# Program order on all engines and later weight conversions in a Mamba-2 scan followed by a low-rank mixer

## Chip, cores, metric

One core of a Trainium2 chip. The metric is the device time of one launch in microseconds (us), median of several executions. Each profile shows one execution; its span, from the first to the last instruction, is some 1.7 us shorter than that execution's time. The granted clock of a stretch is the share of TensorE's full speed that was granted in it: 1.00 is full speed. All runs are fast, save one execution that is named where it occurs. Ratios are the mean time of one kernel's fast runs over that of the other's of the same rounds, so not quite the ratio of the medians quoted.

## The reference

Four batches, eight heads, 768 positions. A chunked state-space scan makes y from x, a, B and C; y becomes a (768 x 256) matrix per batch, and a mixer with weights U, V, w1, w2 follows. The weights come as 64-bit floats and are converted to fp32 on the chip.

```
y[chunk] = (C B^T * L) x + (C state) * decay        # scan, per batch and head
state    = decay_full * state + sum(B x * decay_from_j)
h = y^T @ U @ V ;  u = y + h^T                      # mixer, per batch
out = u + relu(u @ w1) @ w2
```

## The kernel before

The scan works on pairs of 128-row chunks: twelve pairs in all, three per batch (NPR = 3), counted from 0, so that the fourth pair is pair 3. For a pair, `prep` scales B and C with decays (Bs, Cs, bd), `turn` transposes them on TensorE (T), `gram` multiplies them, a VectorE mask gives M, `state` carries S and `wide`, `ychannel` forms y, `ytokens` transposes y back (ytok). The mixer of a batch consists of pieces: `project` (ytok with U, gives pT), `mixed` (pT with V, added to yT), sixteen `up` pieces (w1, relu) and six `down` pieces (w2). All pieces but `mixed` (bank "g") put their products into three PSUM banks "w", which the scan uses too.

```python
    def to_fp32(dst, words):                     # one weight of 64-bit words
        ...                                      # (cut: lo, hi, tmp)
        nc.vector.tensor_scalar(out=e, in0=hi, ...)                       # exponent bits
        nc.scalar.activation(power, e, AF.Relu, bias=bias[:p], scale=8.0)
        nc.vector.scalar_tensor_tensor(out=power, in0=hi, ..., in1=power, ...)
        nc.vector.tensor_scalar(out=top, in0=hi, ...)
        nc.vector.tensor_tensor(out=top, in0=top, in1=power, ...)
        nc.vector.scalar_tensor_tensor(out=rest, in0=lo, ..., in1=power, ...)
        nc.gpsimd.tensor_tensor(out=dst, in0=rest, in1=top, op=ALU.add)
    ...
    with tc.manual_schedule(engines={PE}):       # only TensorE keeps program order
        prep(0); turn(0, 0); turn(0, 1); state(0); gram(0); prep(1)
        pieces = [lambda w=w: to_fp32(*w) for w in weights]   # ten conversions
        for k in range(last + 1):
            ...
            if k: ytokens(k - 1)
            if q == 0 and b:
                some(len(pieces))                # all conversions are done here
                pieces = mixer(b - 1)
                some(2)                          # project, mixed
            ...                                  # prep(k+2), turn(k+1), pieces between
            ychannel(k); state(k + 1); gram(k + 1); some(parts[2])
```

## Time and profile before

| | before |
|---|---|
| time, median of 3 (range) | 294.89 us (294.77 to 295.44) |
| first projection (L403), last part starts | 65.35 us |
| batch 1's projection starts | 127.03 us |
| VectorE busy up to the first projection | 48.44 us |
| TensorE busy up to the first projection | 30.01 us, at clock 0.74 |

Busy time must be read by stretch: over the whole span VectorE is busy 37%, which looks harmless; up to 65 us it is 74%.

### The profile page before, as it was taken

Reading aid. Unit: us, or ns where it says so; the run is one execution under the profiler, and the core shown is the slowest. Engines: PE = TensorE matmul, PEld = TensorE weight load, DVE = VectorE, ACT = ScalarE, POOL = GpSimd, SP = SyncE. Lnnn points to the kernel's source line nnn. Section 1 sums busy time; section 2 is a strip of 40 time slices with the busy share of each in tenths; the row PEclk is TensorE's granted clock in tenths of the full one; section 3 lists DMA queues with packets and bytes.
Section 4 is the critical chain, followed back from the end, with each engine's and each line's share of the span. In section 5 each row is a group of like instructions: output and inputs, shape, how many; then the busy total and the mean of one; then the engine's idle time right before and its main releaser. Section 6 shows DMA issues by size and latency. Waiting matters only on the chain.

```text
span 294.8 us, 5144 instructions
## 1 busy us (share of the span) xinstructions
PE 252.9 (86%) x2238; PEld 193.3 (66%) x2238; DVE 109.2 (37%) x196; ACT 57.1 (19%) x114; POOL 50.9 (17%) x68
## 2 busy tenths in 40 slices
PE   4447631819999999999999999999999998999994
PEld 4436411605778768867788688676886785587583
DVE  2339999794530244034401541325005103200100
ACT  5212331201211121122211221122121111101100
POOL 4333539251401113004011040001000000000000
PEclk9776955775999999999999999999999999999999
DMA  7998889899900100010001000100010001001001
GB/s 91 102 193 294 172 152 112 91 119 96 109 0 0 56 1 2 0 56 2 0 2 53 2 2 0 54 2 2 0 53 2 0 2 53 0 2 53 0 0 53
DMA packets 80950, 14.65 MB, mean 50 GB/s; under 512 B 76000, under 2 KB 79264, under 8 KB 80928
## 3 DMA queue, kind: packets, MB, share of 16 engines
q1 hardware_dynamic: 80928, 14.33, 28.6%
q8 instruction: 17, 0.28, 0.4%
q14 instruction: 5, 0.04, 0.1%
HBM read 11.17 MB, written 3.15 MB: 49 GB/s over the span
## 4 chain that ended last, share of the span: by engine, by line
PE 77%; DVE 9%; SPq 7%; DMA 3%; issue 1%; POOL 1%; ACT 1%; DVEq 0%; POOLq 0%
PE w L424 29%; PE w L440 28%; PE y L374 4%; PE g L310 3%; PE y L367 3%; SPq L94 3%; SPq L93 2%; DVE M L315 2%; PE w L297 2%; DMA words<-in_moe_U_dram 2%; SPq L97 2%; PE w L436 2%; PE w L403 2%; DVE rest L247 2%; PE g L413 2%; DVE power L240 1%
## 5 line engine op out<-in xcount | busy, mean ns | idle before, releaser
L424 PE MATMUL w<-yT,w 128*128 128x384 f32 x256 | 88.7, 497 | 1.1 <-DVE yT L417 1.1
L440 PE MATMUL w<-w,gT 128*128 128x256 f32 x384 | 86.9, 379 | 0.0
L440 PEld LDWEIGHTS w<-w,gT 128*128 128x128 f32 x384 | 71.1, 190 | 8.7
L424 PEld LDWEIGHTS w<-yT,w 128*128 128x128 f32 x256 | 48.0, 193 | 32.0 <-DVE yT L417 2.7
L427 DVE TENSOR_SCALAR gT<-w 128x384 f32<-128x384 f32 x32 | 17.8, 557 | 62.3 <-PE w L424 62.3
L315 DVE TENSOR_TENSOR M<-g,causal 128x1024 int32<-128x1024 int32 x24 | 28.3, 1216 | 3.3 <-PE g L310 3.3
L274 POOL TENSOR_TENSOR Cs<-bc,FC 128x512 f32<-128x512 f32 x12 | 15.5, 1290 | 74.8 <-issue 44.7
L429 ACT ACTIVATE gT<-w 128x384 f32<-128x384 f32 x32 | 15.7, 490 | 56.5 <-PE w L424 56.5
L442 ACT COPY o<-w 128x256 f32<-128x256 f32 x24 | 8.9, 372 | 82.5 <-PE w L440 82.5
L374 PE MATMUL y<-M,x 128*32 128x128 f32 x384 | 15.1, 300 | 6.7 <-DVE M L315 6.7
L349 POOL TENSOR_TENSOR wide<-S,rmask 128x256 f32<-128x256 f32 x20 | 12.8, 653 | 46.9 <-DVE S L344 46.9
L387 DVE COPY ytok<-w 128x512 f32<-128x512 f32 x12 | 8.2, 683 | 31.4 <-PE w L385 31.4
L367 PEld LDWEIGHTS y<-T,wide 128*128 128x128 f32 x80 | 11.4, 205 | 10.8 <-POOL wide L349 8.4
L367 PE MATMUL y<-T,wide 128*128 128x128 f32 x80 | 12.1, 294 | 7.4 <-POOL wide L349 7.2
L300 ACT COPY T<-w 128x512 f32<-128x512 f32 x24 | 13.7, 583 | 24.3 <-PE w L297 24.0
L344 DVE SCALAR_TENSOR_TENSOR S<-S,kept,w 128x32 f32<-128x32 f32 x32 | 6.3, 243 | 31.9 <-PE w L330 17.0
L274 DVE TENSOR_TENSOR Bs<-bc,FB 128x512 f32<-128x512 f32 x12 | 9.3, 776 | 23.6 <-PE w L297 14.6
L374 PEld LDWEIGHTS y<-M,x 128*32 128x32 f32 x384 | 10.6, 118 | 9.3 <-DVE M L315 7.8
L297 PE MATMUL w<-ident,Bs 128*128 128x128 f32 x48 | 10.8, 311 | 6.3 <-DVE Bs L274 5.2
L310 PE MATMUL g<-T 32*128 32x128 f32 x384 | 16.0, 310 | 0.0
L249 POOL TENSOR_TENSOR w<-rest,top 128x512 f32<-128x512 f32 x8 | 12.1, 1508 | 16.0 <-DVE rest L247 15.4
L310 PEld LDWEIGHTS g<-T 32*128 32x128 f32 x384 | 13.6, 212 | 0.6
(68 smaller groups left out, 166.5 us busy)
## 6 DMA issues: line engine op xcount, KB each, us to landing
words<-in_moe_w_ch_dram SPq DMA_DIRECT2D x8, 512.0 KB, 5.4
x<-in_x_dram SPq DMA_DIRECT2D x24, 128.0 KB, 3.8
out_dram<-o SPq DMA_DIRECT2D x8, 384.0 KB, 2.5
bc<-in_B_dram SPq DMA_DIRECT2D x24, 64.0 KB, 3.8
bc<-in_C_dram SPq DMA_DIRECT2D x24, 64.0 KB, 3.6
words<-in_moe_V_dram SPq DMA_DIRECT2D x4, 96.0 KB, 4.8
words<-in_moe_U_dram SPq DMA_DIRECT2D x1, 192.0 KB, 6.0
a_sb<-in_a_dram SPq DMA_DIRECT2D x1, 96.0 KB, 2.0
```

The costliest lines, as they stand in the source:

```text
L274: eng.tensor_tensor(out=t, in0=bc[:, i].rearrange("p c h n -> p (c h) n")[:, :, None, :].to_broadcast(shape), in1=F[:, b, cs].rearrange("p ...
L297: nc.tensor.transpose(out=tp[:, 2 * i + g], in_=flat[:, ts(2 * c + g, P)], identity=ident)
L300: nc.scalar.copy(out=T, in_=tp)
L310: nc.tensor.matmul(out=g_ps[:, r, c, g], lhsT=T[rows, g], rhs=T[rows, 2 + g], start=True, stop=True, skip_group_check=True)
L315: nc.vector.tensor_tensor(out=M[:, :, c].bitcast(INT32), in0=g_ps[:, :, c].bitcast(INT32), in1=causal[:, None, None, :].to_broadcast(sh), ...
L349: nc.gpsimd.tensor_tensor(out=wide, in0=new[:, :, None, :].to_broadcast(wide.shape), in1=rmask[:, None, :, None].to_broadcast(wide.shape), ...
L367: nc.tensor.matmul(out=y[:, c, g], lhsT=wide[:, g].rearrange("p r d -> p (r d)"), rhs=s["T", c][:, 2 + g], start=fresh, stop=False, skip_g ...
L374: nc.tensor.matmul(out=y[ts(r, Q), c, g], lhsT=x_sb[k][:, c, 4 * g + r], rhs=s["M"][:, r, c, g], start=False, stop=True, skip_group_check= ...
L424: nc.tensor.matmul(out=g, lhsT=w1[:, n, ts(m, P)], rhs=uT[:, n, ts(k, HS)], start=(n == 0), stop=(n == NCB - 1))
L427: nc.vector.tensor_relu(gT[k][:, m], g)
L429: nc.scalar.activation(gT[k][:, m], g, AF.Relu)
L440: nc.tensor.matmul(out=o, lhsT=gT[k][:, m, ts(j, P)], rhs=w2[:, m], start=False, stop=(m == NM - 1), skip_group_check=True)
```

## The change

Its intent: let the first mixer start as soon as batch 0 is scanned, and convert each weight only when it is needed. The whole kernel is put in program order, so no scheduler can pull a conversion ahead. The diff, cut to its core:

```diff
+    ctx.enter_context(tc.manual_schedule())                  # all engines
-    for k in range(NPR): load(k)                             # bc and x of batch 0 first
+    load_bc(0); U; load_x(0); load_bc(1); load_x(1); load_bc(2); V; load_x(2); w1 x4; pair 3; w2 x4; rest
     def to_fp32(dst, words):                                 # now a generator in two halves
-        (top: shift and mask; OR power; rest = lo * power; GpSimd adds)
+        nc.vector.tensor_scalar(out=e, ...); nc.vector.tensor_scalar(out=top, ...)
+        nc.scalar.activation(rest, lo, AF.Copy, scale=2.0 ** -32)
+        nc.scalar.activation(power, e, AF.Relu, ...)
+        yield
+        nc.vector.scalar_tensor_tensor(out=rest, in0=top, ..., in1=rest, ...)
+        nc.vector.scalar_tensor_tensor(out=power, in0=hi, ..., in1=power, ...)
+        nc.vector.scalar_tensor_tensor(out=dst, in0=rest, ..., in1=power, ...)
+        yield
-    (decays and keep for all batches at once)
+    (decays and keep for batch 0 first, for the others later)
-        Cs on nc.gpsimd ; ytok on nc.vector ; odd relus on nc.vector
+        batch 0: Cs on nc.vector ; ytok on nc.scalar ; all relus on nc.scalar
-        per half: 8 up pieces, 3 down pieces
+        16 up pieces, then 6 down pieces
+    prep(0); ...; convert(2); state(0); gram(0); prep(1); turn(1, 0); turn(1, 1); decays(others)
+    convert(2); ychannel(0); state(1); gram(1); prep(2); turn(2, 0); turn(2, 1); ytokens(0)
+    convert(2); ychannel(1); state(2); gram(2); convert(2); ytokens(1); ychannel(2); ytokens(2)
+    keep(others)
+    pieces = mixer(0); some(2); convert(1)
+    for _ in range(2): some(2); convert_ahead()
+    prep(3); some(2); convert_ahead(); turn(3, 0); turn(3, 1); some(2)
+    state(3); gram(3); convert_ahead(); some(2); prep(4); convert_ahead(); some(2); convert_ahead()
     (from here the loop over pairs as before)
```

The kernel before has two regimes (stretches in which different engines are the limit), and the change interleaves them: VectorE work leaves a regime that VectorE binds (busy 48.4 of 65.4 us) and goes into one where VectorE was busy 20.6 of 61.7 us.

More of the change, by code (lines that the diff above doesn't have):

```diff
@@ L85, with load_bc @@
     pairs = [(b, q) for b in range(NB) for q in range(NPR)]
-    def load(k):
+    def load_bc(k):
         b, q = pairs[k]
         bc = bc_sb[k] = raw.tile([P, 2, 2, NH, N], FP32, tag="bc", name="bc")
-        xt = x_sb[k] = raw.tile([P, 2, NH, D], FP32, tag="x", name="x")
         for c in range(2):
@@ L94, in load, with load_x @@
             nc.sync.dma_start(out=bc[:, 1, c], in_=C[b, :, sl, :].rearrange("h s n -> s h n"))
+    def load_x(k):
+        b, q = pairs[k]
+        xt = x_sb[k] = raw.tile([P, 2, NH, D], FP32, tag="x", name="x")
         for c in range(2):
@@ L97, in load @@
             nc.sync.dma_start(out=xt[:, c], in_=x[b, :, sl, :].rearrange("h s d -> s h d"))
-    for k in range(NPR):
-        load(k)
     U_sb = const.tile([P, NC, RK], FP32)
@@ L121 @@
     U2, V2, w12, w22 = (w.bitcast(INT32) for w in (moe_U, moe_V, moe_w_ch1, moe_w_ch2))
+    load_bc(0)
     load_words(U_sb, U2.rearrange("(c p) r -> p c r", p=P))
+    load_x(0)
+    load_bc(1)
+    load_x(1)
+    load_bc(2)
     t = words_of(V4[:, None])
@@ L125 @@
         nc.sync.dma_start(out=t[ts(q, RK)], in_=V2[:, ts(q % 2, S)])
+    load_x(2)
     for k in range(DF // WCOLS):
@@ L129 @@
                        w12[ts(c, P), None, ts(k, 2 * WCOLS)])
+    load_bc(3)
+    load_x(3)
     for m in range(0, NM, 2):
@@ L132 @@
                    w22[m * P:(m + 2) * P].rearrange("(m p) d -> p m d", p=P))
-    for k in range(NPR, NB * NPR):
-        load(k)
+    for k in range(NPR + 1, NB * NPR):
+        load_bc(k)
+        load_x(k)
     ident = const.tile([P, P], FP32)
@@ L183 @@
             scalar1=1e-6, scalar2=1.0, op0=ALU.max, op1=ALU.min)
-    la_flat = la.rearrange("p b c h -> p (b c h)")
-    nc.scalar.activation(la_flat, la_flat, AF.Ln)
-    NLA = NB * NC * NH
+    for sl in (slice(0, 1), slice(1, NB)):
+        nc.scalar.activation(la[:, sl], la[:, sl], AF.Ln)
     FB = const.tile([P, NB, NC, NH, 2], FP32)
@@ L192 @@
     nc.vector.memset(FB, 0.0)
-    d = bank("w", 2, NLA)
-    for v in range(2):
-        nc.tensor.matmul(out=d[:, v], lhsT=ref[v], rhs=la_flat, start=True, stop=True)
-    nc.scalar.activation(
-        FC.rearrange("p b c h v -> p v (b c h)"), d, AF.Exp)
-    for v in range(2):
-        hp = slice(64 * v, 64 * v + 64)
-        nc.scalar.activation(
-            FB[hp].rearrange("p b c h v -> p (b c h) v")[:, :, v], d[hp, v], AF.Exp, scale=-1.0)
-    d = bank("w", NB, NC - 1, NH)
-    nc.tensor.matmul(out=d, lhsT=after, rhs=la[:, :, :NC - 1], start=True, stop=False)
@@ L206 @@
-    nc.tensor.matmul(out=d, lhsT=low[0], rhs=la[:, :, 1:], start=False, stop=True)
-    nc.scalar.activation(FD, d, AF.Exp)
-    d = bank("w", NB, NC - 1, NH)
-    nc.tensor.matmul(out=d, lhsT=high, rhs=la[:, :, :NC - 1], start=True, stop=False)
-    nc.tensor.matmul(out=d, lhsT=low[0], rhs=la[:, :, 1:], start=False, stop=True)
-    own = const.tile([P, NB * (NC - 1) * 2, 4], FP32)
-    nc.vector.tensor_tensor(
-        out=own, in0=d.rearrange("p b c (g r) -> p (b c g) r", r=4),
-        in1=rmask[:, None, :].to_broadcast(own.shape), op=ALU.mult)
@@ L216, with decays @@
-    kept_flat = kept.rearrange("p b c g -> p (b c g)")
-    nc.vector.tensor_reduce(out=kept_flat, in_=own, axis=mybir.AxisListType.X, op=ALU.add)
-    nc.scalar.activation(kept_flat, kept_flat, AF.Exp)
+    def decays(bs):
+        n = bs.stop - bs.start
+        d = bank("w", 2, n * NC * NH)
+        for v in range(2):
+            nc.tensor.matmul(out=d[:, v], lhsT=ref[v],
+                             rhs=la[:, bs].rearrange("p b c h -> p (b c h)"),
+                             start=True, stop=True)
+        for v in range(2):
+            hp = slice(64 * v, 64 * v + 64)
+            nc.scalar.activation(
+                FB[hp, bs].rearrange("p b c h v -> p (b c h) v")[:, :, v], d[hp, v], AF.Exp,
+                scale=-1.0)
+        nc.scalar.activation(FC[:, bs].rearrange("p b c h v -> p v (b c h)"), d, AF.Exp)
@@ new lines, in keep @@
+    def keep(bs):
+        n = bs.stop - bs.start
+        d = bank("w", n, NC - 1, NH)
+        nc.tensor.matmul(out=d, lhsT=after, rhs=la[:, bs, :NC - 1], start=True, stop=False)
+        nc.tensor.matmul(out=d, lhsT=low[0], rhs=la[:, bs, 1:], start=False, stop=True)
+        nc.scalar.activation(FD[:, bs], d, AF.Exp)
+        d = bank("w", n, NC - 1, NH)
+        nc.tensor.matmul(out=d, lhsT=high, rhs=la[:, bs, :NC - 1], start=True, stop=False)
+        nc.tensor.matmul(out=d, lhsT=low[0], rhs=la[:, bs, 1:], start=False, stop=True)
+        own = att.tile([P, NB * (NC - 1) * 2, 4], FP32, tag="own", name="own",
+                       bufs=1)[:, :n * (NC - 1) * 2]
+        nc.vector.tensor_tensor(
+            out=own, in0=d.rearrange("p b c (g r) -> p (b c g) r", r=4),
+            in1=rmask[:, None, :].to_broadcast(own.shape), op=ALU.mult)
+        k = kept[:, bs].rearrange("p b c g -> p (b c g)")
+        nc.vector.tensor_reduce(out=k, in_=own, axis=mybir.AxisListType.X, op=ALU.add)
+        nc.scalar.activation(k, k, AF.Exp)
@@ L233, in tmp @@
             return t[:p, :i * j]
-        e = tmp("e", INT32)
+        e, top, power = tmp("e", INT32), tmp("top", INT32), tmp("power", INT32)
+        rest = tmp("rest", FP32)
         nc.vector.tensor_scalar(out=e, in0=hi, scalar1=0x7ff00000, scalar2=None,
                                 op0=ALU.bitwise_and)
-        power = tmp("power", INT32)
+        nc.vector.tensor_scalar(out=top, in0=hi, scalar1=0xfffff, scalar2=0x4b000000,
+                                op0=ALU.bitwise_and, op1=ALU.bitwise_or)
+        nc.scalar.activation(rest, lo.bitcast(UINT32), AF.Copy, scale=2.0 ** -32)
         nc.scalar.activation(power, e, AF.Relu, bias=bias[:p], scale=8.0)
+        yield
+        nc.vector.scalar_tensor_tensor(out=rest, in0=top.bitcast(FP32), scalar=-7.0 * 2 ** 20,
+                                       in1=rest, op0=ALU.add, op1=ALU.add)
         nc.vector.scalar_tensor_tensor(out=power, in0=hi, scalar=-2 ** 31, in1=power,
                                        op0=ALU.bitwise_and, op1=ALU.bitwise_or)
-        top = tmp("top", INT32)
-        nc.vector.tensor_scalar(out=top, in0=hi, scalar1=3, scalar2=0x7ffff8,
-                                op0=ALU.logical_shift_left, op1=ALU.bitwise_and)
-        nc.vector.tensor_tensor(out=top, in0=top, in1=power, op=ALU.bitwise_or)
-        rest = tmp("rest", FP32)
-        nc.vector.scalar_tensor_tensor(out=rest, in0=lo.bitcast(UINT32), scalar=2.0 ** -52,
-                                       in1=power.bitcast(FP32), op0=ALU.mult, op1=ALU.mult)
-        nc.gpsimd.tensor_tensor(out=dst, in0=rest.rearrange("p (i j) -> p i j", i=i),
-                                in1=top.bitcast(FP32).rearrange("p (i j) -> p i j", i=i),
-                                op=ALU.add)
-    bds = []
-    for i in range(2):
-        t = const.tile([P, 2 * NH, 2, N], FP32, name=f"bd{i}")
+        nc.vector.scalar_tensor_tensor(
+            out=dst, in0=rest.rearrange("p (i j) -> p i j", i=i), scalar=2.0 ** -20,
+            in1=power.bitcast(FP32).rearrange("p (i j) -> p i j", i=i),
+            op0=ALU.mult, op1=ALU.mult)
+        yield
+    bds = [const.tile([P, 2 * NH, 2, N], FP32, name=f"bd{i}") for i in range(2)]
+    for t in bds:
         nc.gpsimd.memset(t, 0.0)
-        bds.append(t)
     st = {}
@@ L267, in prep @@
         b, q = pairs[k]
-        bc = bc_sb.pop(k)
+        bc = bc_sb[k]
         s = st[k] = {}
@@ L271, in prep @@
         shape = [P, 2 * NH, 2, N]
-        for i, (name, F, eng) in enumerate((("Bs", FB, nc.vector), ("Cs", FC, nc.gpsimd))):
+        for i, (name, F, eng) in enumerate((("Bs", FB, nc.vector), ("Cs", FC, nc.vector if k < NPR else nc.gpsimd))):
             s[name] = t = att.tile(shape, FP32, tag=name, name=name)
@@ L279, in prep, with decayed @@
                 op=ALU.mult)
-        s["bd"] = bd = bds[k % 2]
+        if k:
+            decayed(k)
+    def decayed(k):
+        b, q = pairs[k]
+        bc = bc_sb.pop(k)
+        st[k]["bd"] = bd = bds[k % 2]
         n = 2 if q < NPR - 1 else 1
@@ L386, in ytokens @@
                                     identity=ident)
-        nc.vector.tensor_copy(
+        copy = nc.scalar.copy if b == 0 else nc.vector.tensor_copy
+        copy(
             out=ytok[b][:, 2 * q:2 * q + 2].rearrange("p c (g d) -> p c g d", g=2), in_=t)
@@ L425, in up @@
                                  start=(n == 0), stop=(n == NCB - 1))
-            if m % 2:
+            if m % 2 and b:
                 nc.vector.tensor_relu(gT[k][:, m], g)
@@ L448, in mixer @@
         pieces = [project, mixed]
+        for half in range(2):
+            for k in range(2):
+                for m in range(half * NM // 2, (half + 1) * NM // 2):
+                    pieces.append(lambda k=k, m=m: up(k, m))
         for k in range(2):
-            for m in range(NM):
-                pieces.append(lambda k=k, m=m: up(k, m))
             for j in range(HT):
@@ L454, in mixer @@
         return pieces
-    with tc.manual_schedule(engines={PE}):
-        last = len(pairs)
-        prep(0)
-        turn(0, 0)
-        turn(0, 1)
-        state(0)
-        gram(0)
-        prep(1)
-        pieces = [lambda w=w: to_fp32(*w) for w in weights]
-        for k in range(last + 1):
-            b, q = divmod(k, NPR)
-            def some(n):
-                for _ in range(min(n, len(pieces))):
-                    pieces.pop(0)()
-            if k:
-                ytokens(k - 1)
-            if q == 0 and b:
-                some(len(pieces))
-                pieces = mixer(b - 1)
-                some(2)
-            if k == last:
-                break
-            quota = -(-len(pieces) // (NPR - q))
-            parts = [quota // 3, quota // 3, quota - 2 * (quota // 3)]
-            if k + 2 < last:
-                prep(k + 2)
-            if k + 1 < last:
-                turn(k + 1, 0)
-                some(parts[0])
-                turn(k + 1, 1)
-            else:
-                some(parts[0])
-            some(parts[1])
-            ychannel(k)
-            if k + 1 < last:
-                state(k + 1)
-                gram(k + 1)
-            some(parts[2])
-        some(len(pieces))
@@ new lines, with convert, convert_ahead @@
+    halves = [half for w in weights for half in (to_fp32(*w),) * 2]
+    def convert(n):
+        for _ in range(n):
+            next(halves.pop(0))
+    def convert_ahead():
+        if len(halves) > 2:
+            next(halves.pop(1))
+        next(halves.pop(0))
+    one, others = slice(0, 1), slice(1, NB)
+    decays(one)
+    prep(0)
+    keep(one)
+    decayed(0)
+    turn(0, 0)
+    turn(0, 1)
+    convert(2)
+    state(0)
+    gram(0)
+    prep(1)
+    turn(1, 0)
+    turn(1, 1)
+    decays(others)
@@ new lines, with some @@
+    convert(2)
+    ychannel(0)
+    state(1)
+    gram(1)
+    prep(2)
+    turn(2, 0)
+    turn(2, 1)
+    ytokens(0)
+    convert(2)
+    ychannel(1)
+    state(2)
+    gram(2)
+    convert(2)
+    ytokens(1)
+    ychannel(2)
+    ytokens(2)
+    keep(others)
+    def some(n):
+        for _ in range(min(n, len(pieces))):
+            pieces.pop(0)()
+    pieces = mixer(0)
+    some(2)
+    convert(1)
+    for _ in range(2):
+        some(2)
+        convert_ahead()
+    prep(3)
+    some(2)
@@ new lines @@
+    convert_ahead()
+    turn(3, 0)
+    turn(3, 1)
+    some(2)
+    state(3)
+    gram(3)
+    convert_ahead()
+    some(2)
+    prep(4)
+    convert_ahead()
+    some(2)
+    convert_ahead()
+    last = len(pairs)
+    for k in range(NPR, last + 1):
+        b, q = divmod(k, NPR)
+        if k > NPR:
+            ytokens(k - 1)
+        if q == 0 and b > 1:
+            some(len(pieces))
+            pieces = mixer(b - 1)
+            some(2)
+        if k == last:
+            break
+        quota = -(-len(pieces) // (NPR - q))
+        parts = [quota // 3, quota // 3, quota - 2 * (quota // 3)]
+        if k + 2 < last:
+            prep(k + 2)
+        if k + 1 < last:
+            turn(k + 1, 0)
+            some(parts[0])
+            turn(k + 1, 1)
+        else:
+            some(parts[0])
+        some(parts[1])
+        ychannel(k)
+        if k + 1 < last:
+            state(k + 1)
+            gram(k + 1)
+        some(parts[2])
@@ L501 @@
+    some(len(pieces))
 _INS = ['x', 'a', 'B', 'C', 'moe_U', 'moe_V', 'moe_w_ch1', 'moe_w_ch2']
```

## The prediction

> **What bounds the kernel now.** I read the busy shares by slice first, then the busy time in three stretches, the chain that ended last around the boundary of the first two, and last the groups and the timeline of VectorE in the first stretch.
>
> ```profile
> PE   4447631819999999999999999999999998999994
> DVE  2339999794530244034401541325005103200100
> PEclk9776955775999999999999999999999999999999
> DMA  7998889899900100010001000100010001001001
> ```
>
> TensorE (PE) is solid from the tenth slice on; VectorE (DVE) is solid in slices 4 to 9, before that. So there are two regimes with a border near 65 us. Busy time by stretch (TensorE, weight loads, VectorE, ScalarE, GpSimd, then granted clock, DMA share, GB/s):
>
> ```profile
> 0.00:65.35 65.35, 30.01 (x446) 24.82 (x447) 48.44 (x90) 16.82 (x29) 30.02 (x42) 0.74 0.93 148
> 65.35:80.00 14.65, 14.27 (x150) 9.31 (x151) 7.29 (x16) 3.00 (x6) 4.38 (x5) 0.76 1.00 107
> 80.00:290.90 210.90, 208.60 (x1643) 159.18 (x1641) 53.47 (x92) 36.96 (x79) 16.49 (x22) 1.00 0.04 14
> ```
>
> From 80 us TensorE is busy 208.6 of 210.9 us at clock 1.00: at most 2.3 us can be won there by ordering. The first 65 us hold 30 us of half-clocked TensorE work and 48.4 us of VectorE work. The chain of waits at the border:
>
> ```profile
> 64.02 0.33 DVE e L236
> 64.36 0.34 DVE top L243
> 64.69 0.61 DVE ytok L387
> 65.35 1.13 PE w L403 x16
> 66.82 1.66 PE g L413 x8
> 69.53 4.02 PE w L424 x8
> 73.99 2.58 PE w L424 x8
> ```
>
> The last token copy of batch 0 (ytok) stands on VectorE behind weight conversions, and the first mixer's projection (L403) starts only after it. Everything after runs at TensorE's pace. So the time is: start of the first projection, plus dense work. What filled VectorE before 65 us:
>
> ```profile
> L315 DVE TENSOR_TENSOR M<-g,causal 128x1024 int32<-128x1024 int32 x8 | 9.4, 1210 | 0.0
> L247 DVE SCALAR_TENSOR_TENSOR rest<-words,power 128x512 f32<-128x512 uint32 x8 | 6.9, 865 | 0.0
> L245 DVE TENSOR_TENSOR top<-top,power 128x512 int32<-128x512 int32 x8 | 6.7, 838 | 0.0
> L240 DVE SCALAR_TENSOR_TENSOR power<-words,power 128x512 int32<-128x512 int32 x8 | 6.7, 852 | 0.0
> L243 DVE TENSOR_SCALAR top<-words 128x512 int32<-128x512 int32 x8 | 5.5, 685 | 1.6 <-POOL w L249 1.6
> L236 DVE TENSOR_SCALAR e<-words 128x512 int32<-128x512 int32 x8 | 3.8, 477 | 0.0
> L249 POOL TENSOR_TENSOR w<-rest,top 128x512 f32<-128x512 f32 x8 | 12.1, 1508 | 16.0 <-DVE rest L247 15.4 <-DVE top L245 0.6
> ```
>
> The eight big conversions cost 6.9+6.7+6.7+5.5+3.8 = 29.6 us of VectorE, or 3.7 us each. Undisturbed ones take 0.34+0.34+0.60+0.60+0.60 = 2.5 us from start to start (timeline, 43 to 45 us). The rest is stretch.
>
> [...] L245 took 1.54 us at 36.95 while GpSimd's L274 ran (itself 1.50 instead of 1.05), and 0.68 at 42.85 with GpSimd idle. [...] granted clock 0.74 before 65 us, and eight L424 matmuls 4.02 us at 69.53 but 2.58 at 73.99. [...] the 18 loads of 64 to 128 KB for batch 0 (rows of 64 or 128 B) go out in 13.2 us, 0.74 each; six of 512 KB in 9.8 us, 1.63 each.
>
> **The change, part by part.** (1) *Conversion.* Five VectorE instructions before, five after (two of one input, three of two): still 2.5 us for a big one undisturbed. GpSimd's addition goes (12.1+1.0+0.6 = 13.7 us), ScalarE gets one more pass, 0.7 us like L239. With GpSimd mostly quiet, the 1.2 us of stretch should nearly vanish. (2) *Lateness.* Only four of ten weights (U, V, two of w1) are converted before the first projection; six move behind it, some 6 x 3.7 = 22 us of VectorE at the old price. To let this pass, the mixers do all sixteen up pieces before the six down pieces. (3) *Rest.* The third batch-0 Cs products go to VectorE (3 x 0.68), batch-0 ytok copies and all batch-0 relus to ScalarE; turn, state and gram of the fourth pair move behind the projection; decays are split.
>
> VectorE before the projection is then: conversions 1.2+2.0+2.5+2.5, masks 3 x 2.3, Bs and Cs 6 x 0.6, states and own 2.5, setup 4: about 25 us. It is no longer the bound; the chain through in-order queues is. I walk it with the durations of the timeline before:
> - la, decays, Bs and Cs (1.3 us) and turns as before: first T about 9.6; x and U (issued at about 3.7 to 5.8) land about 9.7; state 0, gram 0 (2.1 us cold) end 12.2; mask M(0) 2.3 us to 14.5; Bs, Cs of pair 1 to 15.8.
> - VectorE now stands at V. V is issued two x loads earlier than before (15.2 less 1.3, four issues of 0.78, 4.8 to landing): 21. Five us lost, for the queue is in order.
> - V to 23.1, states 0.7, M(1) 2.3, Bs and Cs 1.2: 27.3; turn 2, T to 29.1 on ScalarE, ytok(0), then lo and power for w1 to 31.2; VectorE to 32.5; gram 2 ends 33.5, M(2) 35.8.
> - e of the second w1 comes behind M(2), so ScalarE's power waits for it: 36.8; behind it ytok(1) 37.4, yT(2) 38.0, PE's four transposes 38.7, ytok(2) 39.4. Projection at 39.8 instead of 65.35: 25.5 us earlier.
>
> Then to the next border, batch 1's projection, at 127.03 before: 61.7 us after the first. After: the same plus the fourth pair's turn, state, gram (0.88+0.30+1.10 = 2.3 us warm), plus 0.7 us for 32 of the projection's 48 matmuls that ran early before (56.56), plus stalls. Stalls: six stages of two up pieces. PE needs 2 x 1.29 = 2.6 us a stage, ScalarE 2 x 0.49 + 2 x 0.7 = 2.4, VectorE 2.5. Nearly balanced; but M(3) holds VectorE until gram 3 (about 59 us), so power of the seventh conversion and the relus behind it come late, and three w banks allow three pieces of lead: I take 3 us. 39.8 + 61.7 + 2.3 + 0.7 + 3 = 107.5. The rest is unchanged: 294.8 - 127.0 = 167.8, sum 275.3. I add a little for hops between engines: **276 us**.
>
> Loads: w2's third and fourth wait for the words buffers of w1's two conversions (VectorE 31.8 and 37.7), so pair 4's six loads go out from 39 to 44 and land by 47; prep(4) wants them near 58. At 4.9 us a pair they stay ahead.
>
> **Rivals.** (A) *Conversion takes over as the bound of the first mixer*: the 2.4 to 2.6 us of three engines chain up (e to power to rest to relu to bank) instead of overlapping, 4 us a stage. For: each is in order. Against: conversions are split in halves, one stage ahead. It costs 6 x 1.4 = 8 us: 284. (B) *The scan of batch 0 stays slow*: V lands later or TensorE stays cold, the first projection near 46. For: DMA share is 0.93 there, and the walk has no slack. 282. (C) *Blocked loads*: a late w1 conversion holds the single load queue and pair 4 or 5 comes late; 11 us of margin speaks against; 280 if half goes. (D) *Nothing gained*, because dense work is the bound and gaps only move: the 65 us of half-idle TensorE speak against; 290 or more.
>
> **Range and chances.** My sum leaves 19 us of gain. A or B alone give 282 to 284; both 290. If ScalarE's and VectorE's waits are kinder than walked (V landing at 18), 271. Range 270 to 284. Faster by over 2% needs under 289: 0.95; within 2%: 0.04; slower: 0.01.
>
> **What would show it.** First projection near 40 and batch 1's near 108 (right), or 46 and more (B). TensorE busy over 85% between these two, else A. A VectorE wait of 4 to 5 us for V's load near 16 to 21 us. The 512-wide three-operand conversion instructions near 0.7 us on average rather than 0.85, and VectorE's busy total 5 to 10 us lower. From batch 1's projection to the end 167 to 168 us. If that last stretch is longer than 170, program order has cost something in the steady part, which I count as zero, and the prediction is wrong there.

The marked cuts, here and in the expectations of e_pool and b_upfirst, take out general statements of the hardware that no trace here shows; the numbers measured beside them stand. The 0.7 us added at the end "for hops between engines" are rounding; in the kernel before, the projection started 0.05 us after the copy that released it had ended (65.30, 65.35). "Cold" and "warm" stand for what the granted clock was: in the kernel before, a gram took 2.09 us at 0.50 (from 13.44) and 1.17 us at 1.00 (from 34.14). That the "stretch" comes from GpSimd is inference, from the L245 instructions quoted.

## The result, and the profile after

The changed kernel took 275.29 us (273.10 to 276.23, four runs) beside 295.07 us for the kernel before: ratio 0.9318 (95% interval 0.9262 to 0.9375). In a second call it took 274.08 us, ratio 0.9294. The profiled execution was the fastest of the first four, with a span of 271.4 us; the other three had spans of 273.5 to 274.5.

The same slices as in the prediction, now of the kernel after:

```profile
PE   4673978998999999999999999999999999999994
DVE  4749659697604144362520404342500014120000
PEclk9978899999999999999999999999999999999999
```

TensorE is at seven tenths or more from the fifth slice (27 us) on, where before it was so from the tenth (66 us). VectorE's heavy part lies largely beside it instead of ahead of it. Busy time in the three stretches between the same borders (TensorE, weight loads, VectorE, ScalarE, GpSimd, granted clock, DMA share, GB/s), kernel after:

```profile
0.00:38.02 38.02, 24.11 (x358) 20.90 (x362) 24.25 (x55) 16.19 (x33) 8.71 (x23) 0.91 0.90 170
38.02:103.59 65.57, 62.70 (x633) 47.62 (x636) 35.06 (x63) 23.28 (x47) 12.52 (x18) 1.00 0.62 80
103.59:267.50 163.91, 161.63 (x1268) 121.92 (x1268) 41.02 (x72) 28.26 (x61) 9.34 (x14) 1.00 0.05 15
```

The first projection starts at 38.02 instead of 65.35 us: 27.3 us won. The stretch up to batch 1's projection is 65.57 instead of 61.68 us: 3.9 given back. From there to the end it is 271.4 - 103.6 = 167.8 us, as before (294.8 - 127.0 = 167.8). So -27.3 + 3.9 = -23.4 us, the whole difference of the two spans. It is larger than the 19.8 us between the medians, because the profiled execution of the kernel before was a slower one (296.49 us) and that of the kernel after a faster one (273.10 us); the split holds for these two executions. The chain of waits into the first projection, kernel after:

```profile
15.54 3.92 DMA words<-in_moe_V_dram
20.33 0.56 DVE rest L263
22.54 2.35 DVE M L339 x2
...
34.75 0.72 ACT power L261
35.47 0.47 ACT ytok L412
35.94 0.50 ACT yT L401
36.48 0.66 PE w L409 x4
38.02 1.49 PE w L428 x48
...
41.46 8.01 PE w L449 x24
```

Before, this chain ran through conversions on VectorE up to the last token copy. Now it runs through V's load, the masks, and ScalarE's queue. (V's load is only the last of several waits there: see e_vfirst.) The first 24 up matmuls take 8.01 us, 2.67 per eight: TensorE's granted clock is 1.00 from the first of them on, where before the first eight took 4.02 at a mean of 0.66 (69.53 to 73.55). The conversions' two-input instructions with 512 columns on VectorE (busy us, mean ns), kernel after:

```profile
L267 DVE SCALAR_TENSOR_TENSOR w<-rest,power 128x512 f32<-128x512 f32 x8 | 5.5, 692 | 0.3
L263 DVE SCALAR_TENSOR_TENSOR rest<-top,rest 128x512 f32<-128x512 f32 x8 | 5.5, 686 | 3.1 <-ACT rest L260 3.0
L265 DVE SCALAR_TENSOR_TENSOR power<-words,power 128x512 int32<-128x512 int32 x8 | 5.5, 685 | 0.0
```

The three two-input instructions (the prediction says three-operand) are at 0.69 us instead of 0.84 to 0.87: the lengthening that the prediction calls stretch is gone. VectorE's whole busy time fell from 109.2 to 100.3 us, GpSimd's from 50.9 to 30.6.

### The profile page after: what moved, and what is told of

Read it like the earlier page. It is cut to its first block, busy times and chain, and to the rows that moved or that the text cites. A ratio compares the mean times of both kernels' runs of the same rounds, so it can differ in the third digit from the quotient of the medians.

```text
span 271.4 us, 5196 instructions
## 1 busy us (share of the span) xinstructions
PE 248.4 (92%) x2250; PEld 190.4 (70%) x2250; DVE 100.3 (37%) x190; ACT 68.1 (25%) x141; POOL 30.6 (11%) x55
## 4 chain that ended last, share of the span: by engine, by line
PE 82%; DVE 7%; SPq 5%; ACT 2%; DMA 1%; issue 1%; DVEq 0%
PE w L465 31%; PE w L449 29%; PE g L334 4%; PE y L398 3%; PE w L321 3%; DVE M L339 3%; PE y L391 2%; PE w L428 2%; PE w L461 2%; PE w L409 2%; SPq L94 2%; SPq L95 2%; DMA words<-in_moe_V_dram 1%; PE g L438 1%; SPq L102 1%
## 5 line engine op out<-in xcount | busy, mean ns | idle before, releaser
L449 PEld LDWEIGHTS w<-yT,w 128*128 128x128 f32 x256 | 46.8, 190 | 34.8 <-DVE yT L442 4.1
L454 ACT ACTIVATE gT<-w 128x384 f32<-128x384 f32 x40 | 19.3, 488 | 47.9 <-PE w L449 47.8
L452 DVE TENSOR_SCALAR gT<-w 128x384 f32<-128x384 f32 x24 | 13.4, 558 | 38.2 <-PE w L449 38.2
L412 DVE COPY ytok<-w 128x512 f32<-128x512 f32 x9 | 6.2, 689 | 40.1 <-PE w L409 40.1
L321 PEld LDWEIGHTS w<-ident,Bs 128*128 128x128 f32 x48 | 6.8, 160 | 12.9 <-issue 10.4
L334 PE MATMUL g<-T 32*128 32x128 f32 x384 | 14.7, 291 | 0.0
L398 PE MATMUL y<-M,x 128*32 128x128 f32 x384 | 13.0, 276 | 0.0
L401 ACT COPY yT<-y 128x512 f32<-128x512 f32 x12 | 7.0, 584 | 17.5 <-PE y L398 17.5
L321 PE MATMUL w<-ident,Cs 128*128 128x128 f32 x48 | 10.8, 313 | 0.3 <-DVE Cs L292 0.3
L442 DVE TENSOR_TENSOR yT<-g,yT 128x384 f32<-128x384 f32 x16 | 7.8, 551 | 8.7 <-PE g L438 8.7
```

Source lines behind the costliest of these rows:

```text
L321: nc.tensor.transpose(out=tp[:, 2 * i + g], in_=flat[:, ts(2 * c + g, P)], identity=ident)
L334: nc.tensor.matmul(out=g_ps[:, r, c, g], lhsT=T[rows, g], rhs=T[rows, 2 + g], start=True, stop=True, skip_group_check=True)
L398: nc.tensor.matmul(out=y[ts(r, Q), c, g], lhsT=x_sb[k][:, c, 4 * g + r], rhs=s["M"][:, r, c, g], start=False, stop=True, skip_group_check= ...
L449: nc.tensor.matmul(out=g, lhsT=w1[:, n, ts(m, P)], rhs=uT[:, n, ts(k, HS)], start=(n == 0), stop=(n == NCB - 1))
L452: nc.vector.tensor_relu(gT[k][:, m], g)
L454: nc.scalar.activation(gT[k][:, m], g, AF.Relu)
```

## The experiments

Four calls: the changed kernel itself; then `after_again` to `e_oldloads`; `e_auto` to `b_newconv`; `e_vact` to `b_upfirst`. Where a call has no run of the changed kernel, its ratio to the kernel before (0.9294 and 0.9318 in two calls) is the yardstick. The last three calls ran on different chips, on which the kernel before took 295.26, 294.71 and 295.30 us; so a difference of 1 us between calls is read with care. Names with e_ start from the changed kernel, those with b_ from the kernel before.

**after_again.** No edit.

> The changed kernel as it is, on the chip of these runs, as the yardstick for the three beside it. Expected: 0.93 of the kernel before, as in the first four runs, that is 273 to 276 us; first projection near 38 us, batch 1's near 104, and 167.8 us from there to the end of the span.

Measured 274.08 us (273.90 to 275.39), ratio 0.9294. In its profiled execution the first projection starts at 39.41, batch 1's at 105.8, and 167.8 us follow. Its projection took 2.32 us where the other profile shows 1.52, with the same 48 matmuls; the mean granted clock from there to batch 1's projection was 0.99 instead of 1.00. The kernel after scattered by 1.1% in its first call and by 0.5% in this one, the kernel before by 0.2% and 0.5%. Between the two profiles, whose spans differ by 2.2 us, TensorE was busy 248.4 and 251.7 us with the same 2250 matmuls; the slower projection at the border is all that is seen of the cause, and the slower executions of the first call left no profile.

**e_early.** All conversions ahead of the first mixer.

```diff
-    pieces = mixer(0); some(2); convert(1)
+    convert(12); pieces = mixer(0); some(2)
     (and no convert_ahead() later)
```

> The changed kernel, but all six remaining conversions stand ahead of the first mixer, as the kernel before has them done; everything else as it is. My theory (the gain comes mostly from letting six conversions pass behind the first projection): they cost VectorE 6 x 2.5 to 3 us in one row from about 37 us, and pT and the four additions to yT stand behind them, so the first up pieces start near 54 to 57 us instead of 41.5; the stalls of some 3 us between 56 and 66 us go. Net 9 to 13 us slower than the changed kernel, 284 to 288 us. Rival (the gain comes from the cheaper conversion and the faster scan, and lateness is only cosmetic): at most 4 us slower.

Measured 288.20 us, 14.1 more than the changed kernel (ratio 0.9763): the first theory, a little above its range. TensorE's line at the border, run e_early, with the idle time before it:

```profile
54.48 1.66 PE L438 MATMUL g<-V,pT 32*128 32x384 f32 x8 [14.59 <-ACT pT L431]
```

The projection itself started at 38.38, but `mixed` waited 14.59 us for pT, which stands behind twelve conversion passes on ScalarE, and took 1.66 us instead of the 0.93 of the kernel after. Lateness is the larger part of the gain. The 14.1 us are the price of this one placement, six conversions in a row with TensorE waiting; other early placements were not tried.

**e_pool.** The old formula, with GpSimd's addition, in the new order.

```diff
-        rest: lo * 2^-32 on ScalarE; three scalar_tensor_tensor on VectorE
+        power; top OR power; rest = lo * 2^-52 * power on VectorE; nc.gpsimd.tensor_tensor(out=dst, ..., op=ALU.add)
```

> The changed kernel with the old formula of conversion, whose last addition runs on GpSimd; order and lateness as in the changed kernel. My theory (GpSimd's part mattered [...]and cost VectorE about 1.2 us in each conversion, but in the new order most of that lies beside other work): the three-operand conversion instructions rise from 0.69 us to about 0.8 on average, GpSimd's busy total rises by 12 to 14 us, the wide products wait behind GpSimd's additions; 1 to 4 us slower than the changed kernel. Rival (conversion without GpSimd is the main thing): 8 us or more slower.

Measured 278.77 us, 4.7 more than the changed kernel (0.9463): between the two theories, nearer the first. The first projection hardly moved (39.87 against 39.41); the loss lies in the first mixer, 72.1 instead of 66.4 us (the profiled execution, 281.57 us, was the slowest of the four). Two lines of the waits from 39 to 113 us, run e_pool (total, times, longest):

```profile
POOL w L267 <- DVE rest L265: 24.1, 7, 7.3
PE w L320 <- POOL Cs L291: 3.6, 2, 1.8
```

GpSimd waits in its queue for the next conversion's product, the Cs of the next pair stands behind it, and TensorE's turn waits for that Cs. I had expected VectorE's longer instructions to be the cost; they are there (VectorE's conversion instructions sum to 28.9 us for the eight instead of 24.2), but a queue that waits is the new thing on the path. The run weighs an exchange: with GpSimd's addition back, ScalarE's second pass is gone.

**e_oldloads.** Loads in the order of before.

```diff
-    bc0, U, x0, bc1, x1, bc2, V, x2, w1 x4, pair 3, w2 x4, rest
+    bc0, x0, bc1, x1, bc2, x2, U, V, w1 x4, w2 x4, rest
```

> The changed kernel with the loads in the order of before: the three pairs of batch 0, then U, V, w1, w2, then the rest. My theory (program order makes each queue wait for its next instruction, so U, which VectorE takes before the first states and masks, must land early): VectorE stands from 8.7 us until U lands near 20 us, some 9 us later than in the changed kernel; V then comes almost at once and its wait of 3.8 us goes. First projection 5 to 8 us later, whole time 5 to 8 us slower. Rival (loads are hidden anyway): within 2 us.

Measured 283.36 us, 9.3 more (0.9619): the first theory in kind, more in size. VectorE, run e_oldloads:

```profile
19.85 0.26 DVE L251 TENSOR_SCALAR e<-words 128x192 int32<-128x192 int32 x1 [11.41 <-DMA words<-in_moe_U_dram]
29.57 0.56 DVE L258 SCALAR_TENSOR_TENSOR rest<-top,rest 128x384 f32<-128x384 f32 x1 [3.58 <-ACT rest L255]
```

Waiting for U to land (its data to arrive) costs VectorE 11.4 us: it ran nothing from 8.44 to 19.85. I expected V's wait to vanish; it came back as one for ScalarE (second line). This returns in run e_vfirst. Order of loads and program order belong together: before, VectorE waited only 4.21 us for U, at 20.50, and had done the Bs of pairs 1 and 2 by then.

**e_auto.** Program order on TensorE only.

```diff
-    ctx.enter_context(tc.manual_schedule())
+    ctx.enter_context(tc.manual_schedule(engines={PE}))
```

> The changed kernel, but only TensorE keeps program order; the other engines are ordered by the scheduler, as in the kernel before. Its order puts U's whole conversion ahead of the logarithm and the decays, and draws conversions of w1 and w2 ahead of the mask of the third pair and of the additions to yT. My theory (program order is what lets the conversions pass late): VectorE waits for U to land near 7 to 8 us before anything else, 3 to 4 us lost at once, and first projection falls to 43 to 48 us; 5 to 10 us slower than the changed kernel. Rival (the order of instructions written in the program is enough, and who keeps it doesn't matter): within 2 us.

Measured 279.95 us, ratio 0.9485, some 5 us more than the changed kernel's 0.93: the first theory, at the low end of its range. VectorE in run e_auto waits first of all for U:

```profile
7.78 0.26 DVE L256 TENSOR_SCALAR e<-words 128x192 int32<-128x192 int32 x1 [6.23 <-DMA words<-in_moe_U_dram]
```

The first projection started at 42.77 us, batch 1's 65.65 us later, so the loss lies ahead of the border. The order of statements alone does not do it.

**e_vfirst.** V's four loads ahead of x of pair 1 and B, C of pair 2.

```diff
-    load_bc(1); load_x(1); load_bc(2); V
+    load_bc(1); V; load_x(1); load_bc(2)
```

> The changed kernel with V's four loads moved ahead of pair 1's x and pair 2's B and C. My theory (VectorE's wait of 3.8 us for V stands on the path to the first projection, as predicted): V lands near 15 us, the wait goes, first projection 3 to 3.8 us earlier, near 34.5, and the whole time 2.5 to 3.5 us shorter. Rival (what is won at the start is given back in the first mixer, whose conversions and word buffers do not come earlier): batch 1's projection moves by less than 1.5 us.

Measured 275.87 us, ratio 0.9332: no gain. This is what the rival foretold, but not for its reason: nothing was won at the start that could be given back. V's conversion on VectorE in the kernel after, first half and first instruction of the second (idle time and its end in brackets):

```profile
19.59 0.36 DVE L256 TENSOR_SCALAR e<-words 128x384 int32<-128x384 int32 x1 [3.82 <-DMA words<-in_moe_V_dram]
20.33 0.56 DVE L263 SCALAR_TENSOR_TENSOR rest<-top,rest 128x384 f32<-128x384 f32 x1
```

and in run e_vfirst:

```profile
15.84 0.35 DVE L256 TENSOR_SCALAR e<-words 128x384 int32<-128x384 int32 x1
20.01 0.56 DVE L263 SCALAR_TENSOR_TENSOR rest<-top,rest 128x384 f32<-128x384 f32 x1 [3.55 <-ACT rest L260]
```

V's wait of 3.82 us for the load became one of 3.55 us for ScalarE, and the second half begins only 0.3 us earlier. ScalarE's queue in run e_vfirst tells why: its pass over V stands behind both turn copies and the other batches' decays.

```profile
17.56 0.58 ACT L324 COPY T<-w 128x512 f32<-128x512 f32 x1 [0.27 <-PE w L321]
18.52 0.60 ACT L213 ACTIVATE FB<-w 64x144 f32<-64x144 f32 x2 [0.38 <-PE w L208]
19.13 0.43 ACT L216 ACTIVATE FC<-w 128x288 f32<-128x288 f32 x1
19.44 0.54 ACT L260 ACTIVATE rest<-words 128x384 f32<-128x384 uint32 x1
```

ScalarE kept program order here: V had landed by 15.84 (VectorE read it then), ScalarE stood idle until 16.70 (5.77 us, waiting for TensorE's transposes), and it read V only at 19.44, behind the copies and decays.

**e_vact.** V first, its first half ahead of pair 1's turns, the decays behind pair 1's gram.

```diff
     prep(1)
+    convert(1)
     turn(1, 0); turn(1, 1)
-    decays(others); convert(2)
+    convert(1)
     ychannel(0); state(1); gram(1)
+    decays(others)
```

> The run with V loaded first showed that VectorE's wait of 3.8 us for V's load was replaced by one of 3.6 us for ScalarE, whose pass over V stands behind the turn copies and the decays of the other batches. Here V is loaded first, its first half stands ahead of the turns of pair 1, and the other batches' decays stand behind the gram of pair 1. Theory now (two waits of equal length lay over each other, and TensorE's gram of pair 1 is a third path about 1 us shorter): VectorE's wait for ScalarE in V falls below 1 us, the mask of pair 1 starts near 21.5 instead of 22.6 us, first projection about 1 us earlier; 0.5 to 1.5 us shorter than the changed kernel. Rival (the V wait was the only one and 3 us come out): first projection near 35.

Measured 273.49 us, ratio 0.9260 (0.9238 to 0.9282): about 1 us below the changed kernel's 0.9294 (0.9267 to 0.9322) of another call, as the theory had it, but the intervals overlap and by time alone this is not clear of noise. The trace shows the waits. The second half of V's conversion starts at 16.71 instead of 20.33 us, M(1) at 21.41 instead of 22.54; now TensorE's gram releases it:

```profile
21.41 2.36 DVE L339 TENSOR_TENSOR M<-g,causal 128x1024 int32<-128x1024 int32 x2 [0.34 <-PE g L334]
```

Three paths lay over each other, two of nearly equal length and the third some 1.1 us shorter, and the profile had named one. The rival, 3 us, is out. The first projection came at 38.10, not earlier than in the first profile (38.02), but took 2.33 us instead of 1.52. Against the two runs whose projection was as slow, after_again (2.32 us, at 39.41) and e_vfirst (2.26 us, at 39.80), it came 1.3 and 1.7 us earlier, each a single execution.

**e_stage.** One conversion step ahead of the fourth pair's states.

```diff
-    state(3); gram(3); convert_ahead(); some(2)
+    convert_ahead(); state(3); gram(3); some(2)
```

> The changed kernel with one conversion step moved from behind the fourth pair's states and masks to ahead of them. My theory (the stalls of TensorE between 56 and 66 us, 1.8 us, come from VectorE's queue: it stands 2 us waiting for the fourth pair's states, and the exponent part of the seventh conversion comes after the mask, so ScalarE's queue stands 3.9 us and the relus behind it keep the banks): ScalarE's long wait for the exponent goes, TensorE is busy over 98% from the first up piece to batch 1's projection, 1 to 2.5 us shorter than the changed kernel. Rival (the three engines are simply full there, so a move only moves the stall): within 0.5 us.

Measured 273.76 us, ratio 0.9267 (0.9227 to 0.9307); against 0.9294 of another call this alone would not be clear of noise. The trace is clearer. The stall in the kernel after, first ScalarE, then TensorE:

```profile
58.28 0.72 ACT L261 ACTIVATE power<-e,bias 128x512 int32<-128x512 int32 x1 [3.90 <-DVE e L256]
...
59.43 1.56 PE L449 MATMUL w<-yT,w 128*128 128x384 f32 x4 [0.58 <-ACT gT L454]
62.84 1.56 PE L449 MATMUL w<-yT,w 128*128 128x384 f32 x4 [0.75 <-ACT gT L454]
```

and the stretch from the first to batch 1's projection in run e_stage:

```profile
40.55:104.06 63.51, 62.43 (x629) 48.07 (x628) 35.08 (x63) 23.27 (x47) 12.62 (x18) 0.99 0.59 75
```

63.5 instead of 65.6 us (66.4 in after_again), TensorE busy 62.43 of it (98%) instead of 96%; the 3.90 us wait is gone. Its first projection came at 40.55, later than in both profiles of the kernel after; this lies ahead of the edit, and hides part of the gain in the whole time. The stall was one of order, not of full engines.

**b_newconv.** The kernel before, with the new formula alone.

```diff
-        (old to_fp32 with GpSimd's addition)
+        (new to_fp32, not split in halves)
```

> The kernel before with the new formula of conversion alone, no GpSimd in it; order, loads and lateness as before. My theory: stretch of VectorE's conversions falls from 1.2 us each to near zero, 8 to 10 us less VectorE work before 65 us, but in place of the stretch come waits for ScalarE's second pass; first projection 4 to 9 us earlier, time 4 to 9 us shorter than the kernel before. Rival (before 65 us the kernel is bound by loads and by waits, not by VectorE's work): within 2 us.

Measured 290.25 us, ratio 0.9835: 4.5 us shorter, the low end of the theory. The last part of the first projection starts at 59.34 instead of 65.35; VectorE was busy 44.2 us up to there instead of 48.4, with 90 instructions in both: 4.2 us less, not the 8 to 10 of the theory. Two of the three two-input instructions stayed at 0.79 and 0.73 us on average, and no wait of VectorE for ScalarE's second pass is seen. So the time fell in the range, but two of the steps that led to it did not come.

**b_upfirst.** The kernel before, sixteen up pieces, then six down.

```diff
-        for k: 8 up pieces of k, 3 down pieces of k
+        16 up pieces (four of k = 0, four of k = 1, twice), then 3 down pieces of each k
```

> The kernel before with the mixers' pieces in the new order alone: all sixteen up pieces, then the six down pieces. Theory (the order only makes room for late w2 conversions and costs and wins nothing where all is converted): within 0.7 us of the kernel before, as the 163.9 us that both kernels take from batch 1's projection to TensorE's end say. Rival ([...] better spread of the copies win something): 1.5 us or more shorter.

Measured ratio 0.9983 (0.9956 to 1.0011), fast runs of 294.05 to 295.50 us beside 294.53 to 296.12: nothing, as the theory had it. A further execution, the profiled one, took 1419 us with full clock and was slow; I have no explanation for it, it did not occur again in the other runs of this or any kernel, and nothing is concluded from its trace.

**e_best.** What was learned, together.

```diff
     loads: bc0, U, x0, bc1, V, x1, bc2, x2, ...            # V first
     prep(1); turn(1, 0); turn(1, 1)
-    decays(others); convert(2); ychannel(0); state(1); gram(1)
+    state(1); gram(1); decays(others); ychannel(0)          # masks start early
     prep(2); turn(2, 0); turn(2, 1)
-    ytokens(0); convert(2); ychannel(1); state(2); gram(2); convert(2); ytokens(1)
-    ychannel(2); ytokens(2); keep(others)
+    convert(1); next(halves.pop(1))                         # first halves of V and w1
+    state(2); gram(2); ytokens(0); ychannel(1); convert(2); ytokens(1)
+    ychannel(2); ytokens(2); convert(2)
     pieces = mixer(0); some(2)
+    keep(others)
     (and the step of e_stage)
```

> All that was learned put together: V first; states and gram of the next pair ahead of the y channel of this one in batch 0, so that masks start early; conversion halves of V and the first w1 a pair ahead; keep of the other batches behind the first projection; one conversion step ahead of the fourth pair's states. Theory (the start is a chain through in-order queues in which each mask waits for things that need not be ahead of it): first projection near 33 us, TensorE over 97% busy from there to batch 1's, near 97 to 98 us; 167.8 us after that; 266 to 269 us in all. Rival (cold TensorE and ScalarE's order give it back): first projection 36 or later, 271 or more.

Measured 266.56 us (266.13 to 267.02), ratio 0.9027 (0.9009 to 0.9046): faster than both kernels, by some 8 us than the changed one. Run e_best, the first two stretches:

```profile
0.00:33.40 33.40, 23.50 (x350) 19.25 (x354) 23.06 (x52) 14.14 (x29) 8.72 (x23) 1.00 0.95 164
33.40:97.40 64.00, 62.88 (x640) 48.74 (x644) 37.15 (x67) 25.02 (x51) 12.97 (x18) 1.00 0.66 98
```

The first projection starts at 33.3, batch 1's at 97.3, 167.8 us follow. Each of the three is where the theory put it, and the masks start earlier as meant: M(1) at 20.27 instead of 22.54, M(2) at 26.33 instead of 32.03. The parts of this run were not tried one by one. The clock figure of 1.00 in its first stretch is not to be relied on: the gram at 18.11 took 2.09 us and the one at 25.05 only 1.22.

## Why the prediction was right, point by point

- *What bounds the kernel.* Right, though "half-clocked" was too strong for the first 65 us, with a mean granted clock of 0.74; it was 0.50 from 40 to 55 us. The time is the start of the first projection plus dense work: the part behind batch 1's projection is 167.8 us in both kernels, to the tenth.
- *The walk to the first projection.* It ended at 39.8; the profiles show 38.02 and 39.41. Its stations were near: M(0) ended at 14.6 (walked 14.5), Bs and Cs of pair 1 at 15.8 (15.8), ytok(2) at 37.8 (39.4). Of the 1.8 us, 1.4 came from V, which could be read at 19.6 instead of 21: its four issues took 2.0 us, not 3.1, and it landed 3.9 us after its issue, not 4.8.
- *"Five us lost, for the queue is in order".* The wait was 3.82 us, below the 4 to 5 named as a sign; the reason was incomplete. With V early, 3.55 us were lost to ScalarE's queue (e_vfirst), and with both out of the way TensorE's gram let M(1) start only 1.1 us earlier (e_vact). I walked ScalarE's queue only where the walk needed it, and so did not see that V's pass there stood behind the decays. Had I proposed to load V earlier on this ground, I should have forecast 3 us and got none.
- *The stretch between the two projections.* Forecast 61.7 + 2.3 + 0.7 + 3 = 67.7, measured 65.6. The pair that moved in and the part of the projection that no longer runs early are in it; TensorE's idle time is 2.9 instead of 0.4 us, so 2.5 of the 3 us for stalls. They lie where I put them: VectorE waits for the states and for gram 3, and ScalarE's power of the seventh of the eight 512-column conversions and the relus come late (e_stage). What I left out is TensorE's clock: its busy time is 62.70, and 61.30 + 3.0 would be 64.3, so some 1.6 us (my estimate, the difference of the two) are saved by being at full clock from the first piece (mean granted clock of the stretch 0.94 before, 1.00 after); in after_again, whose projection took 2.32 us, TensorE's busy time is 63.51. I had counted the old slow start again. The 0.7 us for the 32 early matmuls were too few as well: the trace of the kernel before shows 1.08 us for them, so the saving is nearer to 2 us.
- *Conversion.* 0.69 us for the two-input instructions, as forecast (0.7). VectorE 8.9 us lower, in the range of 5 to 10.
- *Loads.* That the loads of small rows (64 or 128 B) move slowly was read from the time between issues, 0.74 us for 64 to 128 KB and 1.63 for 512 KB. This is a loose measure: in the kernel after, four loads of 512 KB went out in 2.27 us, 0.57 each. The bytes moved show it better: in the kernel before 85 to 147 GB/s from 13 to 15 us, while small rows moved, and 376 to 414 from 24 to 27 us, while w1 and w2 did. U (192 KB) took 6.0 us from issue to landing when 19 loads had been issued ahead of it (before), and 3.4 us when five had (after).
- *Rivals.* (A), a stretch of 4 us a stage, did not come: TensorE is 96% busy there, above the 85% named. (B) did not come: 38 to 39.4, not 46. (C): pair 4's six loads went out from 36.9 to 44.1 us (forecast 39 to 44), and no wait of TensorE for loads is seen. (D) is out.
- *The sum.* 275.3 of span was forecast, to be compared with 271.4 in the profile, 273.6 in the second one, and 273.5 to 274.5 in the other three executions of the first call. The forecast time, 276, lies so near the median of 275.29 partly by luck: the walk started from a slower execution of the kernel before, and took 1.8 us too much at V's load and after and 1.6 at the clock. Against this, it added up a span and called it a time: a time is 1.7 us longer, and only 0.7 was added.
- *How the gain splits.* Late conversion is worth 14.1 us (e_early), program order 5 (e_auto), the order of loads 9.3 (e_oldloads), no GpSimd in the conversion 4.7 in the new order (e_pool) and 4.5 in the old (b_newconv), the order of the mixers' pieces nothing by itself (b_upfirst). They sum to more than the 20 us, since each part leans on the others: a late load hurts only in an order that waits for it. Not tried alone: the batch-0 Cs products on VectorE, the ytok copies and relus on ScalarE, the split decays, the conversion in halves.

## What to carry to other kernels

Find the instruction at which the kernel turns from one bound to another, and ask of each piece of work ahead of it whether it has to be there; what need not be goes into the dense stretch, in halves, with the engine order written out. When a wait is to be removed, follow every input of the waiting instruction through the queue of the engine that makes it: two or three waits of equal length may lie over one another, and the profile names only the last. In e_vfirst, a pass of 0.54 us that stood behind copies and decays held VectorE for 3.55 us, almost as long as the late load had (3.82).
